# Attention maxima closed in bursts: the last reduction in one, the transpose between the matmuls of the next, with the maxima 45 steps ahead

## The chip, the cores and the metric

The kernel runs on one core of a Trainium2 chip. The metric is device time in microseconds (us) of one execution; where there are several runs, their median. Smaller is better.

## The reference

The input `x` is 2048 x 640 in float32. Three things are computed from it and mixed row by row:

```
qkv = x @ wqkv                      # 32 heads of 20
a   = softmax(q k^T / sqrt(20)) v   # per head, 2048 x 2048 scores
a   = a @ wo
b   = Re(DFT_seq(DFT_hidden(x)))    # = Cr @ (x Dr^T) - Ci @ (x Di^T)
g   = sigmoid(x . gate_w)
out = g * a + (1 - g) * b
```

## The kernel before, in words

**The work.** There are 16 pairs of heads and two halves of the queries, so 32 units (`NU`), each with two heads and 1024 queries. A unit takes 32 steps. The kernel computes the scores twice. In the maxima pass (`m`, `s_mm`, line 149) a step has two matmuls, one for each head (L159), whose 128 x 512 results VectorE reduces to their row maxima (L161). In the exponential pass (`e`, in `score`, line 664) a step has two matmuls of the transposed scores (L682), with the negated maxima as two extra rows of the query operand, and ScalarE takes their exponentials (L684). The unit's maxima must therefore be in the query operand before its first `e` step. A head uses 64 of the 128 partitions, so an `e` and an `m` matmul on different halves can run beside each other.

**Closing a unit's maxima.** After step 31 of a unit `s_end` (line 163) reduces the 64 partial maxima of a row block to 16 columns on VectorE (L167). At step 1 of the next unit it appends the unit to `chains`, and the next burst calls `max_chain` (line 187): TensorE transposes the 128 x 16 result (L190) into a PSUM bank, VectorE splits it into two parts (`split`, lines 102 and 103), and two steps later SyncE writes the parts to the extra rows of the query operand by four DMAs (lines 198 and 199).

**The prologue.** It projects q, k, v and the gate. 32 `qk_tile` calls (15 x 3 matmuls of 512 columns, L106 to L108, counted by `m`) are left when the maxima begin. Ahead of each third one, `segment` (line 313) computes one tile of the hidden transform (`hid_tile`, 15 pairs of half-height matmuls, L298) and four steps of the maxima pass beside it. `HEAD` is the number of these segments; `LEAD` the number of maxima steps done before the loop starts. The weights of a `qk_tile` are split by `fin()` at the second tile of each group of four.

**The loop.** It has 256 cycles; cycle `c` goes through `ORDER`: eight `e` and eight `m` matmuls, the filling `F`, and at the end the burst `B`. So the maxima pass runs `LEAD` steps ahead of the exponentials, and ends as many steps before the end of the loop. The filling is first the remaining `HID = 64 - HEAD` hidden tiles, one in a cycle, then three cycles with none, then the Fourier transform along the sequence: 56 units of 48 pairs of matmuls (L520), spread evenly over the cycles up to the last but one. The burst (line 688) runs due read-outs of the filling (`run_extras`), two steps of the product of exponentials and v (`av_step`, 8 matmuls each in the trace, L445), and then the chains that wait.

**Order.** Every engine does its instructions in the order in which this code issues them. `at_step(i, fn)` puts work at the begin of step `i` of the `e` pass. What matters here:

- `load_stack` (line 127) gives 12 DMAs for the k and q operands of the next pair of heads, four for k, four for each half of q. `begin` (line 628) puts them on GpSimd's queue (L632) at every second step from step 2 of a pair (64 steps) on. The first eight must have landed before the maxima pass reaches that pair.
- `unit_end` (line 450) copies the unit's output to `o` on ScalarE (L452), a single buffer, and places its normalising at later steps: 27 steps on, GpSimd multiplies (L477), 29 steps on, SyncE stores (L485). The next unit's copy waits for that store.
- `end` (line 644) issues `load_wb` for the weights of hidden tiles 32 to 47 and 48 to 63 when hidden tile 16 or 32 is due (`c + HEAD`), with GpSimd as the splitting engine; and the first loads of the Fourier stage by `HID`. The matrices `a` of that stage are loaded (`load_a`, six buffers `araw`) and split by GpSimd, two for each step from two steps after the last hidden tile on.
- PSUM banks for scores and transposes rotate over five (`bank`, line 112).

Of the kernel before, what the change touches and what calls it, by code (L numbers as in the profile page):

```python
# [10 lines left out]
F32 = mybir.dt.float32  # L11
R = mybir.dt.float32r
AF = mybir.ActivationFunctionType
ALU = mybir.AluOpType
AX = mybir.AxisListType
# [3 lines left out]
P = 128  # L19
# [5 lines left out]
NS = S // P  # L25
# [4 lines left out]
NU = 2 * NP  # L30
# [6 lines left out]
FIRST = {"e": (0, 0, 1, 1), "m": (1, 1, 1, 1)}  # L37


LEAD = 41  # L40
HEAD = 10

# [14 lines left out]
def f32(ap):  # L59
    return ap.bitcast(F32)  # L60
# [3 lines left out]
def mix_kernel(ctx: ExitStack, tc: tile.TileContext, xa, wqk, wb, cdft, wo, out):  # L64
    nc = tc.nc
    pe, act, dve, pool, sp = nc.tensor, nc.scalar, nc.vector, nc.gpsimd, nc.sync
    ctx.enter_context(tc.manual_schedule())

    def pools(**kw):
        return ctx.enter_context(tc.tile_pool(**kw))  # L70

    const = pools(name="const", bufs=1)
    small = pools(name="small", bufs=1)
# [24 lines left out]
    def split(dst1, dst2, src, e1, e2):  # L98
        if e1 is act:
            act.activation(dst1, src, AF.Copy)  # L100
        else:
            e1.tensor_copy(dst1, src)  # L102
        e2.tensor_tensor(dst2, src, f32(dst1), op=ALU.subtract)  # L103
# [8 lines left out]
    def bank():  # L112
        return ps_w.tile([P, 512], F32, name=f"ps{next(turn) % 5}")

    def pair_tile():
        return work.tile([P, 2, 512], F32, name="p", bufs=5)
# [10 lines left out]
    def load_stack(p):  # L127
        kt, qt = kst[p % 2], qst[p % 2]
        u = S // 2
        for t, o, two, one, cs in ((kt, D, 0, 2, slice(0, S)), (qt, 0, 1, 0, slice(0, u)), (qt, 0, 1, 0, slice(u, S))):  # L130
            for h in range(2):
                r = (2 * p + h) * DH
                b = 64 * h
                rows = slice(o + r, o + r + DH)
                yield f32(t[b + two * DH : b + (two + 2) * DH, cs]), qk_scr[:, rows, cs]
                yield f32(t[b + one * DH : b + (one + 1) * DH, cs]), qk_scr[0, rows, cs]

    def q_unit(n):
        u = n % 2 * (S // 2)
        return qst[n // 2 % 2][:, u : u + S // 2]  # L140

    mx, nms, chains = {}, {}, []
    now, later = [-1], {}

    def at_step(i, fn):
        later.setdefault(i, []).append(fn)
# [16 lines left out]
    def s_end(i):  # L163
        n, s = divmod(i, 32)
        if n < NU and s == 31:
            nms[n] = small.tile([P, 16], F32, name="nm", bufs=2)
            dve.tensor_reduce(nms[n], mx.pop(n).rearrange("p h q c -> p (h q) c"), axis=AX.X, op=ALU.max, negate=True)  # L167
        if s == 1 and 0 < n <= NU:
            if now[0] < 0:
                max_chain(n - 1)  # L170
            else:
                chains.append(n - 1)

    def s_step(i):
        for fn in [s_mm(i, h) for h in range(2)]:
# [11 lines left out]
    def max_chain(n):  # L187
        q = q_unit(n)
        pt = bank()[:16, :P]
        pe.transpose(pt, nms.pop(n), ident)  # L190
        m1 = small.tile([16, P], R, name="m1", bufs=2)
        m2 = small.tile([16, P], R, name="m2", bufs=2)
        split(m1, m2, pt, dve, dve)

        def rows():
            for h in range(2):
                b = 64 * h + KROWS
                sp.dma_start(f32(q[b : b + 1, :]), f32(m1[8 * h : 8 * h + 8, :]))
                sp.dma_start(f32(q[b + 1 : b + 2, :]), f32(m2[8 * h : 8 * h + 8, :]))

        if now[0] < 0:
            rows()
        else:
            at_step(now[0] + 2, rows)
# [16 lines left out]
    def load_wqk(c):  # L221
        raw = raw_tile()[:, : ND * P].rearrange("p (d c) -> p d c", d=ND)
        sp.dma_start(raw, wqk[c])

        def finish():
            w = part_tile().rearrange("p z c -> p (z c)")[:, : 2 * ND * P].rearrange("p (z d c) -> p z d c", z=2, d=ND)
            split(w[:, 0], w[:, 1], raw, act, dve)
            wt[c] = w

        return finish  # L230
# [19 lines left out]
    def flush(keep=0):  # L250
        while len(stores) > keep:
            sp.dma_start(*stores.pop(0))
# [60 lines left out]
    def segment(i, steps):  # L313
        def read_out(read, args):
            read()
            stores.append(args)

        tile_ = hid_tile(i, read_out)
        left = 3 * ND
        for k in range(steps):  # L320
            run_s(step + 1)
            for _ in range(left // (steps - k)):
                next(tile_)
                left -= 1
# [3 lines left out]
    def run_s(upto):  # L328
        nonlocal step
        while step < upto:  # L330
            s_step(step)
            step += 1
# [38 lines left out]
    for n, c in enumerate(order):  # L371
        for t in range(4):
            m = 4 * n + t
            if m % 3 == 0 and hid_done < HEAD:
                segment(hid_done, 4)
                hid_done += 1
            qk_tile(c, t)
            if t == 1:
                fin()
                if n + 2 < len(order):  # L380
                    fin = load_wqk(order[n + 2])
    run_s(LEAD)
    flush()
# [55 lines left out]
    def av_step(i, n, kt):  # L439
        v = vts[n // 2]  # L440
        pp = [pts.pop((n, kt, qc)) for qc in range(2)]
        for qc in range(2):
            for h in range(2):
                j = 2 * qc + h
                pe.matmul(av[32 * j : 32 * j + DH + 1, :], v[:, kt, h * (DH + 1) : (h + 1) * (DH + 1)],  # L445
                          pp[qc][:, h, :], start=kt == 0, stop=kt == NS - 1)
        if kt == NS - 1:
            unit_end(i, n)

    def unit_end(i, n):  # L450
        o = pa.tile([P, 512], F32, name="o")
        act.activation(o, av, AF.Copy)  # L452
        lc = pa.tile([P, 16], F32, name="lc")
        rb = pa.tile([P, 512], F32, name="rb")

        q = pool if n == NU - 1 else sp

        def store_l():
            for j in range(4):
                r = 32 * j + DH  # L460
                q.dma_start(l_scr[n, j : j + 1], o[r : r + 1, :])

        def load_l():
            q.dma_start(lc, l_scr[n].rearrange("j (a b) -> (j a) b", b=16))

        def recip():
            dve.reciprocal(lc, lc)

        def store_r():
            q.dma_start(r_scr[n].rearrange("j (a b) -> (j a) b", b=16), lc)  # L470

        def load_r():
            for j in range(4):
                q.dma_start(rb[32 * j : 32 * j + 32, :], r_scr[n, j : j + 1].to_broadcast([32, 512]))

        def norm():
            pool.tensor_tensor(o, o, rb, op=ALU.mult)  # L477

        def store_o():
            for qc in range(2):  # L480
                for h in range(2):
                    j = 2 * qc + h
                    t0 = (n % 2) * (S // 2) + qc * 512
                    r = (2 * (n // 2) + h) * DH
                    q.dma_start(o_scr[r : r + DH, t0 : t0 + 512], o[32 * j : 32 * j + DH, :])  # L485

        steps = (1, 5, 14, 16, 20, 27, 29) if n < NU - 2 else (1, 4, 10, 12, 15, 19, 21)
        for k, fn in zip(steps, (store_l, load_l, recip, store_r, load_r, norm, store_o)):
            if n == NU - 1:
                rest.append(fn)  # L490
            else:
                at_step(i + k, fn)
# [84 lines left out]
    def start_dft():  # L577
        flush()
        proj.release()
        apool.append(pools(name="apool", bufs=1))  # L580
# [19 lines left out]

    HID = 4 * NS - HEAD
    fills = itertools.chain(*(hid_tile(HEAD + g, read_later) for g in range(HID)), itertools.chain.from_iterable(dft_step(g) for g in range(NS * UNITS)))

# [24 lines left out]
    def begin(i):  # L628
        now[0] = i
        n, s = divmod(i, 32)  # L630
        for fn in later.pop(i, ()):
            fn()  # L632
        if s % 2 == 0:
            flush()
        if s == 0 and n % 2 == 0:
            p = n // 2
            if p + 1 < NP:
                at_step(i + 6, functools.partial(load_v, p + 1))
                for j, args in enumerate(load_stack(p + 1)):
                    at_step(i + 2 + 2 * j, functools.partial(pool.dma_start, *args))  # L640
        if i < total:
            pts[n, s // 2, s % 2] = pair_tile()

    def end(i):
# [3 lines left out]
        if i % 4 == 2:  # L648
            c = i // 4
            if c + HEAD in (NS, 2 * NS):  # L650
                load_wb(3 + (c + HEAD) // NS, pool, pool)()
            if c in (HID - 5, HID - 3):
# [8 lines left out]

    heads = {"e": 0, "m": 2 * LEAD}

    def score(kind):
        x = heads[kind]
        heads[kind] += 1
        i, z = divmod(x, 2)
        h = z ^ FIRST[kind][(i - (LEAD if kind == "m" else 0) - 1) % 4]
        if kind == "m":
# [17 lines left out]

    def burst(c):
        run_extras(max(done - HIDS, 0) // 3, 2)
        for kt in (2 * c, 2 * c + 1):  # L690
            av_step(now[0], kt // NS, kt % NS)
        while chains:
            max_chain(chains.pop(0))
        if c == HID - 1:
            start_dft()

# [89 lines left out]
```

## Time and profile before

| | |
|---|---|
| median of 3 runs | 1979.33 us (1977.02 to 1981.08) |
| the profiled execution | 1972.39 us |
| its span in the trace | 1970.6 us |
| TensorE (PE) busy | 1928.0 us, 98% |
| VectorE (DVE) busy | 1454.8 us, 74% |
| ScalarE (ACT) busy | 1212.2 us, 62% |
| GpSimd (POOL) busy | 1097.4 us, 56% |

A timeline row gives the start and the length in us, the engine, the line, the operation, `out<-in` with shapes, and the number of instructions merged. What stands in brackets is how long the engine was idle before it, and whose end ended that. A row of several instructions has the time from the first's start to the last's end. PE is matmuls, PEld their weight loads; SPq rows are DMA issues of SyncE. In the rows of groups the columns are busy us, mean ns, and the idle time before them.

### The profile page before, as it was taken

How to read it: one execution, taken by the hardware profiler on the slowest of the kernel's cores; microseconds unless marked ns; L12 is line 12 of the kernel's file. 1: busy time of each engine (PE TensorE's matmuls, PEld its weight loads, DVE VectorE, ACT ScalarE, POOL GpSimd, SP SyncE). 2: the span in 40 equal slices, each digit the busy share in tenths (PEclk: the TensorE clock that was granted, in tenths of full speed). 3: DMA queues.
4: the chain of work that ended last, by engine and by line, in shares of the span. 5: the costliest groups of instructions: out<-in, count | busy, mean ns of one | idle time of the engine just before them, and what ended most of it. 6: DMA issues, size and time to landing. Idle time of an engine off the chain costs nothing. (4 is left out here: it accounts for less than half of the span.)

```text
span 1970.6 us, 43800 instructions
## 1 busy us (share of the span) xinstructions
PE 1928.0 (98%) x17080; PEld 1384.3 (70%) x17080; DVE 1454.8 (74%) x2419; ACT 1212.2 (62%) x2337; POOL 1097.4 (56%) x1010
## 2 busy tenths in 40 slices
PE   8999999999999999999999999999999999999998
PEld 7987767767775666666676666666666666666678
DVE  4144569988887887888888878888888888888323
ACT  4221147767776666667776767677677666767741
POOL 1210001111004999756479987996686789787534
PEclk9999999999999999999999999999999999999999
DMA  7663321312114565436356646664555566553355
GB/s 222 172 170 132 131 91 46 84 51 72 51 51 133 181 195 161 121 111 159 101 152 191 194 151 186 195 191 125 153 175 137 172 182 184 147 169 128 102 158 177
DMA packets 196511, 281.02 MB, mean 143 GB/s; under 512 B 73373, under 2 KB 137917, under 8 KB 194385
## 3 DMA queue, kind: packets, MB, share of 16 engines
q1 hardware_dynamic: 158992, 246.20, 40.6%
q0 software_dynamic: 37312, 32.03, 6.5%
q8 instruction: 134, 2.20, 0.5%
q14 instruction: 73, 0.59, 0.1%
HBM read 213.81 MB, written 63.70 MB: 141 GB/s over the span
## 5 line engine op out<-in xcount | busy, mean ns | idle before, releaser
L161 DVE TENSOR_REDUCE mx<-ps 128x1 f32<-128x512 f32 x2048 | 1288.3, 684 | 210.4 <-PE ps L159 191.8
L684 ACT ACTIVATE p<-ps 128x512 f32<-128x512 f32 x2048 | 1081.0, 599 | 451.8 <-PE ps L159 244.4
L159 PE MATMUL ps<-kst,qst 60*128 60x512 f32 x2048 | 778.3, 428 | 19.6 <-ACT p L684 8.9
L682 PE MATMUL ps<-qst,kst 62*128 62x512 f32 x2048 | 705.2, 424 | 3.7 <-DMA qst<-m 2.2
L520 PE MATMUL yp<-a,part 64*128 64x320 f32 x5376 | 689.9, 310 | 0.1
L520 PEld LDWEIGHTS yp<-a,part 64*128 64x128 f32 x5376 | 595.2, 187 | 15.5 <-DVE m L540 0.3
L445 PE MATMUL av<-p,v 128*21 128x512 f32 x4096 | 493.3, 597 | 0.1
L682 PEld LDWEIGHTS ps<-qst,kst 62*128 62x128 f32 x2048 | 339.1, 185 | 212.6 <-DVE mx L161 179.3
L159 PEld LDWEIGHTS ps<-kst,qst 60*128 60x128 f32 x2048 | 366.0, 185 | 51.2 <-ACT p L684 12.3
L103 POOL TENSOR_TENSOR part<-raw,part 128x1024 fp32r<-128x1024 f32 x112 | 267.3, 2387 | 9.0
L445 PEld LDWEIGHTS av<-p,v 128*21 128x21 f32 x4096 | 98.2, 100 | 226.3 <-issue 222.7
L298 PE MATMUL yp<-wb,xs 64*128 64x320 f32 x1920 | 239.8, 312 | 2.1 <-ACT raw L306 1.9
L298 PEld LDWEIGHTS yp<-wb,xs 64*128 64x128 f32 x1920 | 208.9, 189 | 7.1 <-ACT raw L306 2.5
L416 POOL TENSOR_TENSOR raw<-raw,raw 128x1024 f32<-128x1024 f32 x78 | 187.8, 2408 | 9.4 <-DMA raw<-in_cdft 9.1
L551 POOL TENSOR_TENSOR yt<-yt,m 128x320 f32<-128x320 f32 x64 | 56.2, 879 | 146.9 <-DVE m L540 146.6
L102 POOL CAST wb<-raw 128x966 fp32r<-128x966 f32 (+1 forms) x4 | 3.4, 856 | 228.6 <-DMA raw<-in_wb 196.7
L102 POOL CAST part<-raw 128x1024 fp32r<-128x1024 f32 x112 | 116.3, 1039 | 18.3 <-PE yp L520 12.5
L477 POOL TENSOR_TENSOR o<-o,rb 128x512 f32<-128x512 f32 x32 | 41.5, 1296 | 133.7 <-DMA rb<-r_scr 131.5
L103 POOL TENSOR_TENSOR a<-araw,a 128x320 fp32r<-128x320 f32 x112 | 97.7, 872 | 9.0
L103 DVE TENSOR_TENSOR p<-ps,p 128x512 fp32r<-128x512 f32 x40 | 27.5, 691 | 94.9 <-ACT p L100 92.1
L106 PE MATMUL ps<-xs,part 128*128 128x512 f32 x200 | 80.3, 402 | 7.5 <-ACT xs L100 6.2
L100 ACT ACTIVATE p<-ps 128x512 fp32r<-128x512 f32 x40 | 23.8, 597 | 102.5 <-PE ps L108 102.4
(68 smaller groups left out, 1389.0 us busy)
## 6 DMA issues: line engine op xcount, KB each, us to landing
raw<-in_cdft SPq DMA_DIRECT2D x192, 512.0 KB
araw<-a_scr SPq DMA_DIRECT2D x192, 160.0 KB
qk_scr<-p SPq DMA_DIRECT2D x40, 512.0 KB
y_scr<-yt SPq DMA_DIRECT2D x96, 160.0 KB
kst<-qk_scr POOLq DMA_DIRECT2D x32, 320.0 KB, 14.1
qst<-qk_scr POOLq DMA_DIRECT2D x64, 160.0 KB, 8.7
a_scr<-raw SPq DMA_DIRECT2D x64, 160.0 KB
yt<-y_scr SPq DMA_DIRECT2D x64, 160.0 KB
```

Source lines behind the costliest of these rows:

```text
L102: e1.tensor_copy(dst1, src)
L103: e2.tensor_tensor(dst2, src, f32(dst1), op=ALU.subtract)
L106: pe.matmul(ps, st1, mv1, start=first, stop=False)
L159: pe.matmul(ps, q[b : b + KROWS, qt * P : (qt + 1) * P], k[b : b + KROWS, kc * 512 : (kc + 1) * 512], start=True, stop=True)
L161: return lambda: dve.tensor_reduce(mx[n][:, h, qt, kc : kc + 1], ps, axis=AX.X, op=ALU.max)
L298: pe.matmul(yp[h][:, :HE], xs[r, xz, d, cs], w[r, wz, d, :HE], start=d == 0 and z == 0, stop=d == ND - 1 and z == 2)
L416: pool.tensor_tensor(raws[0], raws[0], raws[1], op=ALU.add if PRODUCTS[n][0][1][0] > 0 else ALU.subtract)
L445: pe.matmul(av[32 * j : 32 * j + DH + 1, :], v[:, kt, h * (DH + 1) : (h + 1) * (DH + 1)], pp[qc][:, h, :], start=kt == 0, stop=kt == NS - 1)
L520: pe.matmul(yp[h][:, :HE], c[r, cz, cs], a[r, az], start=s == 0 and z == 0, stop=s == NS - 1 and z == 2)
L551: pool.tensor_tensor(y, y, m, op=ALU.add if sg > 0 else ALU.subtract)
L682: pe.matmul(pt, k[b : b + KROWS + 2, kt * P : (kt + 1) * P], q[b : b + KROWS + 2, qc * 512 : (qc + 1) * 512], start=True, stop=True)
L684: act.activation(pts[n, kt, qc][:, h], pt, AF.Exp, scale=float(DH) ** -0.5)
```

## The change

`LEAD` goes from 41 to 45 and `HEAD` from 10 to 11, so one more segment stands in the prologue, and one hidden tile fewer in the loop. The closing reduction becomes a function of its own, `max_nm`; in the loop `s_end` only notes that the unit is due (`ends`). The next burst calls `max_nm` ahead of its matmuls and, one step later, moves the unit to `chains`, so that the burst after it calls `max_chain`, now between its two `av_step`s instead of after them. With the pass 45 steps ahead, the unit's last maxima come one cycle earlier than before, and the transpose falls into the same burst (after step 24 of the unit in the `e` pass) as before. The 12 loads of `load_stack` are placed 1.5 steps apart, from step 2 to step 18 instead of 24.

```
-LEAD = 41
-HEAD = 10
+LEAD = 45
+HEAD = 11
...
     def s_end(i):
         n, s = divmod(i, 32)
         if n < NU and s == 31:
-            nms[n] = small.tile([P, 16], F32, name="nm", bufs=2)
-            dve.tensor_reduce(nms[n], mx.pop(n).rearrange("p h q c -> p (h q) c"), axis=AX.X, op=ALU.max, negate=True)
-        if s == 1 and 0 < n <= NU:
             if now[0] < 0:
-                max_chain(n - 1)
+                max_nm(n)
             else:
-                chains.append(n - 1)
+                ends.append(n)
+        if s == 1 and 0 < n <= NU and now[0] < 0:
+            max_chain(n - 1)
+
+    def max_nm(n):
+        nms[n] = small.tile([P, 16], F32, name="nm", bufs=2)
+        dve.tensor_reduce(nms[n], mx.pop(n).rearrange("p h q c -> p (h q) c"), axis=AX.X, op=ALU.max, negate=True)
...
-                    at_step(i + 2 + 2 * j, functools.partial(pool.dma_start, *args))
+                    at_step(i + 2 + 3 * j // 2, functools.partial(pool.dma_start, *args))
...
     def burst(c):
         run_extras(max(done - HIDS, 0) // 3, 2)
-        for kt in (2 * c, 2 * c + 1):
-            av_step(now[0], kt // NS, kt % NS)
+        while ends:
+            max_nm(ends[0])
+            at_step(now[0] + 1, functools.partial(chains.append, ends.pop(0)))
+        av_step(now[0], 2 * c // NS, 2 * c % NS)
         while chains:
             max_chain(chains.pop(0))
+        av_step(now[0], (2 * c + 1) // NS, (2 * c + 1) % NS)
```

2 lines of the change are left out of this document (1 added, 1 removed).

## Prediction

> **What bounds the kernel now.** I read the page first, for the busy shares.
>
> ```profile
> span 1970.6 us, 43800 instructions
> PE 1928.0 (98%) x17080; PEld 1384.3 (70%) x17080; DVE 1454.8 (74%) x2419; ACT 1212.2 (62%) x2337; POOL 1097.4 (56%) x1010
> L161 DVE TENSOR_REDUCE mx<-ps 128x1 f32<-128x512 f32 x2048 | 1288.3, 684 | 210.4 <-PE ps L159 191.8
> ```
>
> TensorE is never seen idle for long, yet its matmuls overlap, so 98% does not say that it sets the pace. The timeline does. The loop has 256 cycles; each ends in a burst of 16 L445 matmuls, so the distance between two L445 rows is the length of a cycle. In the Fourier stage, where a cycle is filled with 12 or 16 pairs of L520 matmuls, I took one stretch of each kind:
>
> ```profile
> 1384.49 1.92 PE L445 MATMUL av<-p,v 128*21 128x512 f32 x16
> 1390.73 1.91 PE L445 MATMUL av<-p,v 128*21 128x512 f32 x16
> ...
> 1397.04 1.91 PE L445 MATMUL av<-p,v 128*21 128x512 f32 x16
> 1403.11 1.47 PE L445 MATMUL av<-p,v 128*21 128x512 f32 x10
> ```
>
> ```profile
> 1026.96 1.92 PE L445 MATMUL av<-p,v 128*21 128x512 f32 x16
> 1033.33 1.91 PE L445 MATMUL av<-p,v 128*21 128x512 f32 x16
> ...
> 1039.84 1.91 PE L445 MATMUL av<-p,v 128*21 128x512 f32 x16
> 1046.12 1.47 PE L445 MATMUL av<-p,v 128*21 128x512 f32 x9
> ```
>
> The first stretch has 12 pairs a cycle, the second 16. The plain cycles (the last of each) take 6.07 and 6.28 us: four more pairs cost only 0.21 us. Something else than TensorE's work limits the 12-pair cycle. VectorE's timeline shows what:
>
> ```profile
> 1389.44 0.22 DVE L167 TENSOR_REDUCE nm<-mx 128x16 f32<-128x64 f32 x1
> ...
> 1399.45 4.98 DVE L161 TENSOR_REDUCE mx<-ps 128x1 f32<-128x512 f32 x8 [1.10 <-PE ps L682]
> ```
>
> The eight maxima of a cycle run end to end for 4.98 us, then VectorE rests 1.10 us, while TensorE is in its burst and makes no scores. So a cycle is a chain: maxima back to back, then the burst. **Whatever VectorE does between two maxima is paid; what it does during the burst, up to that rest, is not; and whatever lengthens the burst is paid.** Where no maxima are left, at the end of the loop, a 12-pair cycle takes 4.74 us:
>
> ```profile
> 1846.86 1.92 PE L445 MATMUL av<-p,v 128*21 128x512 f32 x16
> 1851.60 1.91 PE L445 MATMUL av<-p,v 128*21 128x512 f32 x16
> ```
>
> **The change, part by part.** Times are against the profiled execution, 1972.39 us (span 1970.6), which is 6.94 us under the median of the three runs, 1979.33. I work out a difference and add it to the median.
>
> *The closing reduction (L167) moves into a burst.* The row 1389.44 lies inside the cycle 1384.49 to 1390.73, which is 6.24 long against 6.07 plain: 0.17. With 16 pairs: 1026.96 to 1033.33 is 6.37 against 6.28: 0.09. With a hidden-transform tile (15 L298 pairs) as filling:
>
> ```profile
> 299.06 1.92 PE L445 MATMUL av<-p,v 128*21 128x512 f32 x16
> 305.31 1.91 PE L445 MATMUL av<-p,v 128*21 128x512 f32 x16
> 311.67 1.91 PE L445 MATMUL av<-p,v 128*21 128x512 f32 x16
> ```
>
> 6.36 against 6.25: 0.11. In the burst it stands behind the last maxima, and even where the read-out of a tile shares that rest, 0.42 us of it is left:
>
> ```profile
> 307.72 2.61 DVE L161 TENSOR_REDUCE mx<-ps 128x1 f32<-128x512 f32 x4 [0.42 <-PE ps L159]
> ```
>
> So its 0.22 is covered; without that cover it would cost what it costs now. How often it runs:
>
> ```profile
> L167 DVE TENSOR_REDUCE nm<-mx x32: 220/220/221, 222.3 to 1840.5; 128x16 f32<-128x64 f32 x32
> ```
>
> Of the 32, the first stands in the prologue, and the last ones touch the end of the maxima or one of the disturbed cycles below; I count 29, by the filling of their cycles: 14 x 0.17 + 8 x 0.09 + 7 x 0.11 = **-3.9 us**.
>
> *The transpose (L190) goes between the two steps of the burst.* Today its cycle, 1390.73 to 1397.04, takes 6.31 against 6.07, with 16 pairs 6.51 against 6.28. In the new place its wait for the reduction is gone, but that wait was not what ended last. TensorE's weight loads around one transpose:
>
> ```profile
> 834.48 0.12 PEld L445 LDWEIGHTS av<-p,v 128*21 128x21 f32 x4 [0.31 <-issue]
> 834.90 0.12 PEld L445 LDWEIGHTS av<-p,v 128*21 128x21 f32 x4 [0.31 <-issue]
> 835.87 0.09 PEld L190 LDWEIGHTS ps<-ident,nm 128*16 128x16 f32 x1 [0.85 <-DVE mx L161]
> 836.08 0.18 PEld L682 LDWEIGHTS ps<-qst,kst 62*128 62x128 f32 x1
> ```
>
> Inside the burst the loads come every 0.42 us, one group of four ahead, so the last group starts at about 835.33. The transpose's load is not drawn ahead: it comes 0.54 after that, 0.12 later than a next group would. It holds TensorE for 0.21. (The maximum named as releaser was long done; the load stands behind the burst.) Between the two steps there are two such ends of a group train instead of one, so I add 0.11 to the 0.21: burst 0.43 + 0.54 + 0.21 + 0.43 + 0.54 = 2.15 against 2.04. VectorE's two copies of the transpose then fall into its rest, but today's 6.31 is 0.24 over plain, of which TensorE's 0.21 is nearly all, so little is gained. 31 transposes x 0.11 = **+3.4 us**. The bounds: -0.9 (31 x the 0.03 of the copies, if the place itself were free) and +6.5 (the whole 0.21 once more).
>
> The Trainium skill ("TensorEngine Tiling (Array Packing)", Key Properties) says that a change of tiling mode drains the engine; by it the edit adds one drain per unit, and the 0.12 above agrees with that.
>
> *The eleventh segment.* A hidden-transform tile and four steps of maxima move from the loop into the prologue. What a segment costs there, and what stands at the place where the new one goes (ahead of tile 30 of 32):
>
> ```profile
> 215.70 0.40 PE L108 MATMUL ps<-xs,part 128*128 128x512 f32 x1
> ...
> 220.31 0.50 PE L106 MATMUL ps<-xs,part 128*128 128x512 f32 x1
> ...
> 220.89 0.39 PE L108 MATMUL ps<-xs,part 128*128 128x512 f32 x1
> ```
>
> ```profile
> 260.74 0.40 PE L108 MATMUL ps<-xs,part 128*128 128x512 f32 x1
> 262.45 0.50 PE L106 MATMUL ps<-xs,part 128*128 128x512 f32 x1 [1.31 <-ACT part L100]
> ...
> 263.31 0.51 PE L108 MATMUL ps<-xs,part 128*128 128x512 f32 x1
> ```
>
> These matmuls follow each other at 0.23, so a segment adds 220.31 - 215.70 - 0.23 = 4.38. At the new place TensorE already waits for weights that ScalarE and VectorE are still splitting: 262.45 - 260.74 - 0.23 = 1.48, and 0.28 more at 263.31 (0.86 from the restart against 0.58 at 220.31). The segment covers that: 4.38 - 1.76 = **+2.6**.
>
> In the loop one hidden cycle (6.25) becomes a Fourier cycle. 199 of them instead of 198 share the same 56 units of 48 pairs; units take 3 cycles of 16 or 4 of 12, so 78 sixteen-pair cycles become 75: 6.07 - 3 x 0.21 - 6.25 = **-0.8**. The maxima end a cycle earlier, so one more cycle runs without them: 4.74 - 6.07 = **-1.3**.
>
> *The filling moved a cycle earlier against the units.* The longest cycle of the hidden stage:
>
> ```profile
> 417.57 0.91 SPq L237 DMA_DIRECT2D raw<-in_wb  x2
> ...
> 427.87 1.42 SPq L485 DMA_DIRECT2D o_scr<-o  x4
> ```
>
> ```profile
> 421.17 0.99 POOL L102 CAST wb<-raw 128x966 fp32r<-128x966 f32 x1 [31.91 <-PE ps L159]
> ...
> 426.55 1.29 POOL L477 TENSOR_TENSOR o<-o,rb 128x512 f32<-128x512 f32 x1
> ```
>
> ```profile
> 425.02 1.92 PE L445 MATMUL av<-p,v 128*21 128x512 f32 x16
> ...
> 430.64 0.60 ACT L452 ACTIVATE o<-av 128x512 f32<-128x512 f32 x1 [4.17 <-DMA o_scr<-o]
> ...
> 431.78 0.49 PE L159 MATMUL ps<-kst,qst 60*128 60x512 f32 x1 [3.21 <-ACT p L684]
> ...
> 436.39 1.06 PE L445 MATMUL av<-p,v 128*21 128x512 f32 x8
> ```
>
> Read backwards: TensorE waits for an exponential, ScalarE for the store of the unit's output `o`, the store for GpSimd's normalising (L477), and that stood behind GpSimd's split of weights, whose load went out at 417.57. The cycle takes 11.37, 5.1 over 6.25. With one tile fewer in the loop, `load_wb` comes four steps (6.2 us) earlier, the normalising stays at its step, and GpSimd's 5.4 us of splitting end before it. **-5.1 us**; between -5.1 and 0.
>
> *The stack loads (L632) at 1.5 steps instead of 2.* The eighth, the last that the next pair's first maximum needs, goes from step 16 to 12, and that maximum from 23 to 19: seven steps both times. I cost it at zero, but GpSimd must reach the place four steps sooner; the last rival prices that.
>
> Sum: -3.9 + 3.4 + 2.6 - 0.8 - 1.3 - 5.1 = **-5.1 us**: 1974.2 on the median, 1967.3 for an execution like the profiled one.
>
> **Rivals.**
>
> *The transpose is free between the steps* (chance 0.12). Its load could be drawn under the first step and the second step's under the transpose. Against it: neither its load nor the scores' load behind it is drawn ahead in the rows above. Then the 3.4 goes, and with the hidden copies 0.9 more: 1969.9. The Trainium skill ("TensorE: Matmul & The Clock Gate", Part 2) says that loads into the background weight buffer are pulled ahead of running matmuls; that would give this case.
>
> *The long wait only moves* (0.16). At the start of the Fourier stage, also a cycle earlier, a unit's output store comes in SyncE's queue behind 14 loads of `araw` instead of six, and these wait for GpSimd to free six buffers. If that delays ScalarE there as the weights did, 5 us come back: 1979.3, no change.
>
> *Slower: GpSimd reaches the stack loads too late* (0.22). Today this already happens:
>
> ```profile
> 620.65 2.78 POOL L632 DMA_DIRECT2D qst<-qk_scr  x5
> ...
> 623.14 0.54 PE L159 MATMUL ps<-kst,qst 60*128 60x512 f32 x1 [2.28 <-DMA qst<-qk_scr]
> ```
>
> GpSimd takes its instructions in order and each load costs it 0.56; eight in 10 steps instead of 14, among its splits. The load landed 2.5 us after its issue; from there every us of lateness is a us of TensorE. If GpSimd is busy without a rest, moving a load past four steps of its work brings it forward by less than 6.2 us. A shortfall of 1 us in each of the 12 pairs of the Fourier stage gives +12: 1986. It decides when the eighth load is issued under 2.5 us ahead of the pair's first maximum.
>
> **How the numbers follow.** The forecast has 0.50, the rivals 0.12, 0.16 and 0.22. A measurement here tells about 0.2% (4 us) from no change. The forecast lies just beyond it; its own range is 1968 to 1980 (the transpose at its bounds, the weights' stall between gone and half left), so of its 0.50 I give 0.32 to faster, 0.16 to same, 0.02 to slower. The free transpose is faster, the moved wait 0.11 same and 0.05 slower, the late loads slower save 0.01. Together: faster 0.44, same 0.28, slower 0.28. The range from 1965 to 1988 reaches from the free transpose, a little further, to the late loads.
>
> **What would show it.** Right: L167 inside the burst and its cycle at plain length; a burst with the transpose about 2.15 us up to the next score's load; no wait of TensorE near 262; the split of `wb` over before L477, and no 11-us cycle there. Wrong: second-step L445 loads ahead of the transpose's end; an 11-us cycle a few cycles into the Fourier stage; waits on `qst<-qk_scr` longer and in more pairs than now.

## The result: about 17 us slower, and the profile after

The changed kernel takes 1994.95 us (median of 6 runs, 1992.62 to 1999.29) against 1977.74 us for the kernel before, run beside it (6 runs, 1971.16 to 1981.08). The ratio is 1.0098 (95% interval 1.0076 to 1.0120). The profiled execution took 1993.63 us, 21.2 more than the one shown of before. In the code after, lines up to 165 keep their numbers and those quoted from later on move by 3, apart from the closing reduction: `av` is L448, the exponentials L687, the stack loads L635, the transpose L193; the closing reduction is L175.

From the page of the changed kernel (busy time and share by engine; two groups, whose columns are busy us, mean ns, idle time before them and what ended most of it):

```profile
PE 1939.0 (97%) x17080; PEld 1380.6 (69%) x17080; DVE 1457.1 (73%) x2419; ACT 1211.4 (61%) x2337; POOL 1097.1 (55%) x1010
L161 DVE TENSOR_REDUCE mx<-ps 128x1 f32<-128x512 f32 x2048 | 1289.7, 685 | 240.0 <-PE ps L159 221.5
L159 PE MATMUL ps<-kst,qst 60*128 60x512 f32 x2048 | 780.3, 430 | 34.7 <-DMA qst<-qk_scr 18.6
```

The work is the same: VectorE's maxima take 1289.7 us as they took 1288.3. What grew is the idle time before them, from 210.4 to 240.0, and the last row names a cause at the end of the chain: L159 itself, the matmuls of the maxima pass, waited for a DMA of the stacks.

The timeline says where in the span the time was lost. The loop's first burst starts at 282.24 us after and at 280.35 before, so in these two executions 1.9 us are lost ahead of the loop. From the first burst to the last the loop takes 1628.70 us against 1608.56, 20.1 more; after it the kernel gains 0.9. To split the loop I took the length of each of its 256 cycles, the median of each kind (filling, with or without the reduction or the transpose), and what single cycles lie over the median of their kind. That excess is 49.1 us after and 29.6 before. **So 19.5 of the loop's 20.1 us are in some 16 disturbed cycles, and the other 240 are as long as before within a few us in all.**

Of the waits of TensorE (total us, times, longest), these name them. After, then before:

```profile
PE ps L159 <- DMA qst<-qk_scr: 18.6, 4, 6.9
PE ps L159 <- DVE mx L161: 10.1, 7, 3.2
```

```profile
PE ps L159 <- DMA qst<-qk_scr: 4.6, 3, 2.3
```

Four long waits for `qst`, the query half of a pair's stack, stand at the first maximum of pairs 4, 9, 11 and 14 (counted from 0):

```profile
617.11 0.76 PE L159 MATMUL ps<-kst,qst 60*128 60x512 f32 x1 [6.91 <-DMA qst<-qk_scr]
...
1132.53 0.76 PE L159 MATMUL ps<-kst,qst 60*128 60x512 f32 x1 [4.35 <-DMA qst<-qk_scr]
...
1347.82 0.76 PE L159 MATMUL ps<-kst,qst 60*128 60x512 f32 x1 [3.66 <-DMA qst<-qk_scr]
...
1653.88 0.76 PE L159 MATMUL ps<-kst,qst 60*128 60x512 f32 x1 [3.65 <-DMA qst<-qk_scr]
```

At the first maximum of a pair TensorE waits 18.9 us in all, against 7.0 before: +11.9. The cycles there and the ones behind them lie 32.1 us over their medians, against 10.3: +21.8. All other disturbed cycles together: 17.0 after, 19.3 before. Of the 21.8, some 20 are the stack loads': the four waits above and the cycles behind them cost 27.8, the three waits for `qst` in the kernel before 7.6. Of the other cycles there, after the change 4.2 us (pairs 5, 8 and 10) come behind a wait of VectorE's for the sums of the softmax. This is the loss, and the rest of the document is about two questions: why the loads come late, and why 11.9 us of waiting cost 21.8.

**One pair, read closely.** GpSimd's issues of the stack loads of pair 9, after and before. The eight that the first maximum needs are the four of `kst` and the first four of `qst`:

```profile
1106.72 1.25 POOL L635 DMA_DIRECT2D kst<-qk_scr  x2
1110.30 0.66 POOL L635 DMA_DIRECT2D kst<-qk_scr  x1
...
1116.88 0.53 POOL L635 DMA_DIRECT2D kst<-qk_scr  x1
1117.40 0.64 POOL L635 DMA_DIRECT2D qst<-qk_scr  x1
1121.18 1.69 POOL L635 DMA_DIRECT2D qst<-qk_scr  x3
```

```profile
1107.47 1.25 POOL L632 DMA_DIRECT2D kst<-qk_scr  x2
1111.01 1.18 POOL L632 DMA_DIRECT2D kst<-qk_scr  x2
1120.44 1.17 POOL L632 DMA_DIRECT2D qst<-qk_scr  x2
1124.76 0.65 POOL L632 DMA_DIRECT2D qst<-qk_scr  x1
1131.35 0.53 POOL L632 DMA_DIRECT2D qst<-qk_scr  x1
```

The issue of the eighth ends 9.0 us earlier after the change (1122.87 against 1131.35 plus 0.53), as intended. It lands at 1132.53, when TensorE's wait ends: only 1.4 us before the 1133.90 at which the first maximum ran before. From the first issue to the eighth landing it takes 25.8 us. The place of the first load is step 2 both times, and the first maximum stands at step 64 - LEAD: 21 steps behind the first load with LEAD 41, 17 with 45. A step is a quarter of a cycle, 1.56 us: **32.8 us of room before, 26.5 after, of which GpSimd's lateness takes 5** (step 2 of the pair began at 1101.77).

The same sum holds for the other pairs of the Fourier stage. In pairs 9, 11 and 14 GpSimd issues the first load 5.0, 4.8 and 3.9 us behind the begin of step 2, so that 21.5, 21.7 and 22.6 us are left, and the eight need 25.6, 25.1 and 26.0 until they have landed: these three wait. In pair 5 GpSimd is as late (5.1), but there the cycle before had already lost 3.2 us, and only 0.3 of waiting are left. In the other pairs from 6 on it is at most 2.2 us late, the eight take 20.6 to 26.8 us, and TensorE does not wait.

**Pair 4, with the longest wait, is another case.** It lies where the Fourier matrices begin. GpSimd issued its first load at 577.07, and then stood before the sum of two such matrices (L419), which waited for its data:

```profile
577.07 0.67 POOL L635 DMA_DIRECT2D kst<-qk_scr  x1 [16.87 <-PE ps L159]
590.35 2.40 POOL L419 TENSOR_TENSOR raw<-raw 128x1024 f32<-128x1024 f32 x1 [12.61 <-DVE mx L161]
...
596.25 1.67 POOL L635 DMA_DIRECT2D kst<-qk_scr  x3
...
609.86 3.38 POOL L635 DMA_DIRECT2D qst<-qk_scr  x6
```

The eighth is the second of the last row, issued at 610.50, when TensorE was ready for the first maximum since 610.20 (617.11 - 6.91). Here the place of the first load says little; GpSimd came too late to the others. In the kernel before the same stand cost 2.28 us of waiting (623.14, a row of the prediction). So 4.6 of the 11.9 us are pair 4's.

**What a long gap costs beyond itself.** By windows of the changed kernel around the same wait (stretch; its length and the busy us of PE, PEld, DVE, ACT and POOL; then the granted clock, the DMA engines' busy share, GB/s):

```profile
1120.00:1128.00 8.00, 8.00 (x78) 5.88 (x74) 6.90 (x13) 6.01 (x13) 7.77 (x10) 1.00 0.81 220
1132.50:1134.50 2.00, 1.97 (x12) 2.00 (x14) 1.17 (x2) 0.00 (x0) 1.94 (x4) 0.50 0.49 103
...
1140.00:1148.00 8.00, 8.00 (x81) 5.70 (x79) 7.47 (x15) 5.97 (x13) 7.86 (x6) 1.00 0.27 88
```

```profile
1123.54 1.92 PE L448 MATMUL av<-p,v 128*21 128x512 f32 x16
1135.17 3.16 PE L448 MATMUL av<-p,v 128*21 128x512 f32 x16
1142.50 1.06 PE L448 MATMUL av<-p,v 128*21 128x512 f32 x8
```

After the gap TensorE runs on half the clock: the burst takes 3.16 us where it took 1.92. The cycle with the wait takes 11.63, 5.55 over the 6.08 of its kind, and the next one 7.33, 1.22 over: 6.8 us for a gap of 4.35. The first row shows something else: while the eight loads were under way, the DMA engines were busy for 81% and moved 220 GB/s. The Trainium skill ("TensorE: Matmul & The Clock Gate", Part 1) says that the clock falls to half after an idle window of about 3.4 us and rises again after as long a busy one; the 0.50 after gaps of 3.65 to 6.91 us and the 1.00 from 1140 on agree. But 3.4 us is no threshold here: shorter gaps were followed by half the clock too, the one of 2.42 us before 717.24 by 0.50 from 717.9 to 721.3, and in the kernel before that of 2.28 us before 623.14 by 0.50 from 623.4 to 626.8. Over the four pairs the cycles lost 27.8 us (8.4, 6.8, 5.9 and 6.7) for 18.6 us of gaps.

### The profile page after: what moved, and what is told of

Read it like the earlier page. It is cut to its first block, busy times and chain, and to the rows that moved or that the text cites. A ratio compares the mean times of both kernels' runs of the same rounds, so it can differ in the third digit from the quotient of the medians.

```text
span 1991.7 us, 43795 instructions
## 1 busy us (share of the span) xinstructions
PE 1939.0 (97%) x17080; PEld 1380.6 (69%) x17080; DVE 1457.1 (73%) x2419; ACT 1211.4 (61%) x2337; POOL 1097.1 (55%) x1010
## 5 line engine op out<-in xcount | busy, mean ns | idle before, releaser
L161 DVE TENSOR_REDUCE mx<-ps 128x1 f32<-128x512 f32 x2048 | 1289.7, 685 | 240.0 <-PE ps L159 221.5
L687 ACT ACTIVATE p<-ps 128x512 f32<-128x512 f32 x2048 | 1080.4, 599 | 479.8 <-PE ps L159 251.2
L159 PE MATMUL ps<-kst,qst 60*128 60x512 f32 x2048 | 780.3, 430 | 34.7 <-DMA qst<-qk_scr 18.6
L448 PE MATMUL av<-p,v 128*21 128x512 f32 x4096 | 508.0, 607 | 0.1
L159 PEld LDWEIGHTS ps<-kst,qst 60*128 60x128 f32 x2048 | 366.5, 186 | 67.5 <-issue 23.7
L448 PEld LDWEIGHTS av<-p,v 128*21 128x21 f32 x4096 | 95.9, 101 | 216.6 <-issue 209.0
L419 POOL TENSOR_TENSOR raw<-raw,raw 128x1024 f32<-128x1024 f32 x78 | 187.8, 2408 | 13.6 <-DMA raw<-in_cdft 9.7
L102 POOL CAST part<-raw 128x1024 fp32r<-128x1024 f32 x112 | 116.4, 1039 | 23.4 <-PE yp L523 18.0
L103 DVE TENSOR_TENSOR p<-ps,p 128x512 fp32r<-128x512 f32 x40 | 27.5, 691 | 92.2 <-ACT p L100 89.5
L635 POOL DMA_DIRECT2D qst<-qk_scr x120 | 69.4, 591 | 28.8 <-DMA kst<-qk_scr 27.5
## 6 DMA issues: line engine op xcount, KB each, us to landing
kst<-qk_scr POOLq DMA_DIRECT2D x32, 320.0 KB, 15.7
```

What stands on the lines that cost most here:

```text
L159: pe.matmul(ps, q[b : b + KROWS, qt * P : (qt + 1) * P], k[b : b + KROWS, kc * 512 : (kc + 1) * 512], start=True, stop=True)
L161: return lambda: dve.tensor_reduce(mx[n][:, h, qt, kc : kc + 1], ps, axis=AX.X, op=ALU.max)
L419: pool.tensor_tensor(raws[0], raws[0], raws[1], op=ALU.add if PRODUCTS[n][0][1][0] > 0 else ALU.subtract)
L687: act.activation(pts[n, kt, qc][:, h], pt, AF.Exp, scale=float(DH) ** -0.5)
```

## The experiments

**My theory**, once the traces lay side by side: the lead (45) takes four steps from the time between the first stack load and the first maximum, and the 25 us that eight loads need no longer fit. Its rival: the new spacing of the loads is the culprit, since it crowds GpSimd's queue. Others: the transpose in the burst costs more than the rows of before showed; the reduction in the burst delays the transpose. Times are medians, each against runs of the kernel before on the same chip, whose median was 1973.9 to 1974.8 in these sessions.

**1. The lead alone** (kernel before):

```
-LEAD = 41
-HEAD = 10
+LEAD = 45
+HEAD = 11
```

> The kernel before with the maxima 45 steps ahead and eleven segments, and nothing else: closing and transpose as before, loads of the next pair of heads every second step. Theory A (headroom): the eight loads that a pair's first maximum needs take some 25 us from the first issue at step 2; with 19 steps instead of 23 until they are needed, TensorE waits. Here the eighth is placed at step 16, only three steps before, so the waits on these loads are at least those of the change (excess of disturbed cycles 49 us there, 30 before), and the kernel is 15 to 40 us slower than before. Theory B (density): the loads 1.5 steps apart are what delays; then this kernel has no more waits on them than before and lies within 5 us of it, on the fast side by the 5 us of the weights' stall. Theory C (the filling moved by a cycle): the waits lie elsewhere than at a pair's first maximum.

Measured: 2051.55 us, ratio 1.0385 [1.0363, 1.0407]: 77 us slower.

```profile
PE ps L159 <- DMA qst<-qk_scr: 64.8, 10, 11.8
```

The lead, with the eleventh segment that goes with it here, is the culprit, and far beyond what I expected of it (15 to 40 us); experiments 9 and 10 take the two apart. TensorE waits 68.6 us at the pairs' first maxima, and the excess of disturbed cycles is 104.1 us.

**2. The change with the old spacing of the loads:**

```
-                    at_step(i + 2 + 3 * j // 2, functools.partial(pool.dma_start, *args))
+                    at_step(i + 2 + 2 * j, functools.partial(pool.dma_start, *args))
```

> The changed kernel with the loads of the next pair at every second step again, all else changed. Theory A: worse than the change by 5 to 30 us, since the eighth load comes at step 16 for a first maximum at step 19. Theory B: back to the kernel before or below it (0 to -5 us).

Measured: 2059.32, ratio 1.0426 [1.0404, 1.0449]. The denser spacing is no cause of the loss: it takes 64 us of it back.

**3. The new spacing alone** (the kernel before with `3 * j // 2`).

> The kernel before with the loads 1.5 steps apart and nothing else: maxima still 41 steps ahead, first needed at step 23. Theory A: the loads have seven steps more than in the change after the last of the eight; no wait on them longer than before, some shorter: 0 to -10 us. Theory B: 10 to 20 us slower, as the change.

Measured: 1968.16, ratio 0.9969 [0.9954, 0.9983]. At the old lead the denser loads are a gain of some 6 us; TensorE's waits at the pairs' first maxima fall from 7.0 us to 0.4. The rival is out.

**4. The transpose between the `av` steps, alone:**

```
-        for kt in (2 * c, 2 * c + 1):
-            av_step(now[0], kt // NS, kt % NS)
+        av_step(now[0], 2 * c // NS, 2 * c % NS)
         while chains:
             max_chain(chains.pop(0))
+        av_step(now[0], (2 * c + 1) // NS, (2 * c + 1) % NS)
```

> The kernel before with the transpose between the two steps of the burst instead of after them; the closing reduction stays where it was. If the second end of a group train costs 0.13 us for each of 31 transposes, as the changed trace suggests: +4 us (3 to 5), the transpose's cycle 0.12 to 0.13 longer than in the kernel before. If the longer transpose cycle of the change has another cause (the reduction's new place), 0 to 1 us.

Measured: 1978.42, ratio 1.0018 [1.0005, 1.0031]: 3.6 us slower. Its cycles with a transpose take 6.57, 6.43 and 6.64 us (hidden tile, 12 pairs, 16 pairs) where the kernel before takes 6.45, 6.31 and 6.52: 0.12 each, 31 times 3.7.

**5. The reduction in a burst, alone** (the transpose stays behind the burst):

```
     def burst(c):
+        while ends:
+            max_nm(ends.pop(0))
         run_extras(max(done - HIDS, 0) // 3, 2)
```

> The kernel before with the closing reduction at the head of the burst in whose cycle the unit ends, and the transpose after the two steps of that same burst as before; maxima 41 steps ahead, loads as before. If the reduction is covered by VectorE's rest in the burst: its cycles at plain length (6.10 instead of 6.25 with 12 pairs, 6.25 instead of 6.37 in the hidden stage), -4 us (-3 to -5) by the undisturbed cycles. Rival: the transpose in the same burst now waits for the reduction, which stands behind the last maxima; then its cycle grows by 0.3 us or more and the sum is +5 us or more.

Measured: 1971.32, ratio 0.9985 [0.9964, 1.0006], some 3 us faster, though the interval touches no change. What it says for sure is in the cycles: those with the reduction take 6.24, 6.09 and 6.31, which is the plain length; those with the transpose are unchanged.

**6. The changed kernel with the loads still denser** (`i + 1 + j`: one in each step, from step 1 on).

> The changed kernel with the 12 loads at every step from step 1 on (eighth at step 8 instead of 12). If the wait is set by when the eighth load is issued (lateness of GpSimd): the waits at a pair's first maximum go, excess of disturbed cycles from 49 to some 25 us, -20 us against the change, at or under the kernel before. If it is set by a fixed time of some 25 us from the first issue to the eighth landing: only the one step by which the first comes earlier is gained, 1.6 us a pair where it waits, -5 to -12 us against the change, still above the kernel before.

Measured: 1998.86, ratio 1.0118 [1.0084, 1.0151]: no gain, where both branches of the expectation had one. Pair 9 again, GpSimd's issues and the first maximum, and then GpSimd's and TensorE's waits:

```profile
1109.14 2.39 POOL L635 DMA_DIRECT2D kst<-qk_scr  x4
...
1120.44 1.69 POOL L635 DMA_DIRECT2D qst<-qk_scr  x3
```

```profile
1134.58 0.76 PE L159 MATMUL ps<-kst,qst 60*128 60x512 f32 x1 [3.98 <-DMA qst<-qk_scr]
```

```profile
POOL qst L635 <- DMA kst<-qk_scr: 86.2, 39, 7.9
```

```profile
PE ps L159 <- DVE mx L161: 19.7, 8, 6.7
PE ps L159 <- DMA qst<-qk_scr: 9.8, 3, 4.1
```

The four of `kst` go out without a pause, and the eighth lands 25.4 us after the first issue, against 25.8 with the wider spacing. **In the Fourier stage some 25 us is what the eight loads need, and no spacing of mine made it shorter** (medians over pairs 5 to 15: 25.4 in the changed kernel, 25.7 here, 30.8 with two steps' spacing in experiment 1). Nor does the first load go out earlier for its earlier place: in pair 9 it is again 5.0 us behind the begin of step 2. What the dense spacing does instead is to hold GpSimd: a load waits for an earlier one to land, 86.2 us in all against 27.5 in the changed kernel, and the splits and read-outs behind it come late. The waits at the pairs' first maxima fall to 9.8, and others rise as much.

**7. The loads on SyncE's queue** (`sp.dma_start` in place of `pool.dma_start`, in the changed kernel).

> The changed kernel with the 12 loads on SyncE's queue instead of GpSimd's, at the same steps. If the time to land comes of GpSimd's own queue and of its lateness: the eighth lands under 6 us after its issue, no waits at a pair's first maximum, excess from 49 to 25 us or less. If the transfers themselves are what takes 10 us (the DMA engines are shared): same landing times, same waits. If SyncE comes too late to them because it stands behind stores that wait: the waits move to other places or grow.

Measured: 2094.64, ratio 1.0596 [1.0555, 1.0636], the slowest of all.

```profile
PE ps L159 <- DMA qst<-qk_scr: 48.3, 13, 5.3
PE ps L159 <- DVE mx L161: 47.8, 14, 6.3
```

The time is no answer: as I read it, what a stack load waits for on SyncE the matrix stream and the stores behind it wait for too, and the second row shows waits that are not for the stacks at all. SyncE also takes 20 to 30 us to issue the eight, where GpSimd takes 13 (median). But from the eighth's issue to the first maximum, at which TensorE waits in every pair from 5 to 15, it is 10.5 us (median; 7.7 to 12.2), and in the changed kernel the eighth lands 10.6 us after its issue (median; 9.1 to 14.8). So the landing is as slow on this queue, which speaks against GpSimd's queue as the cause. It is not a clean test, since the matrix stream is in SyncE's queue as well.

**8. The kernel before with the two parts that gain**: loads at 1.5 steps, reduction in the burst; lead 41, ten segments, transpose behind the burst (the edits of 3 and 5).

> The kernel before with two parts of the change that cost nothing there: loads 1.5 steps apart (measured alone: ratio 0.997) and the reduction in the burst, transpose after both steps, maxima 41 steps ahead, ten segments. If the two add up: -6 -4 = -10 us against the kernel before, ratio 0.995, about 1964.

Measured: 1965.93, ratio 0.9949 [0.9931, 0.9966]. Faster than both kernels.

**9. The same with eleven segments**, the last with one step of maxima in place of four, so that the lead stays 41.

> The kernel before with three parts of the change: loads 1.5 steps apart, the reduction in the burst, and an eleventh segment that takes a hidden tile out of the loop but only one step of maxima with it, so that the maxima stay 41 steps ahead; transpose after both steps. Against the kernel with the first two (ratio 0.995 to before): the cycle in which GpSimd's split of weights held up the normalising (5 us over) should be plain, the segment costs about 2 in the prologue and gives back 0.8 in the loop: -3 to -5 us more, about 1962, ratio 0.993. Rival: the filling a cycle earlier brings other waits of the Fourier stage and nothing is left: ratio 0.995 or above.

Measured: 1971.39, ratio 0.9982 [0.9970, 0.9994], so the eleventh segment loses 5 us here. The weights' cycle of 11.4 us is gone, as intended: the bursts there start at 416.49, 422.75 and 429.06. But waits come up elsewhere. One kind comes with the eleventh segment: VectorE waits in the loop for the sums of the softmax (`lc<-l_scr`) here, in experiment 10 and in the changed kernel (7.6 us in three places there), and in none of the kernels with ten segments. The first two rows of TensorE's waits, where experiment 8 has 6.3 us for exponentials and 1.7 for maxima:

```profile
PE ps L159 <- ACT p L690: 14.1, 6, 4.8
PE ps L159 <- DVE mx L161: 9.6, 6, 3.2
```

The excess of disturbed cycles is 33.9 us against 23.4. So moving the filling by one cycle against the units removes one meeting of GpSimd, a store and ScalarE, and others come up; which stream makes each of them I did not test.

**10. The changed kernel with a lead of 43**; the eleventh segment has three steps of maxima, the others four:

```
-LEAD = 45
+LEAD = 43
...
-                segment(hid_done, 4)
+                segment(hid_done, 4 if hid_done < 10 else 3)
```

> The changed kernel with the maxima 43 steps ahead instead of 45, all else changed; the last segment has three steps. The first maximum of a pair then comes at step 21, 19 steps (29.7 us) after the loads' place. If some 25 us of transfers and up to 5 us of GpSimd's lateness are what has to fit: the waits nearly go, excess of disturbed cycles from 49 to 30 or less, -15 to -22 us against the change, near the kernel before. If the waits come with the eleventh segment or the new place of closing: no change against the changed kernel.

Measured: 1975.57, ratio 1.0004 [0.9990, 1.0017], 19 us back.

```profile
PE ps L159 <- DMA qst<-qk_scr: 3.8, 3, 2.9
```

The eight loads take 25.2 us as before. Two steps, 3.1 us more of room, and the waits at the pairs' first maxima fall from 18.9 to 4.0, of which 2.95 are pair 4's. This is the sharpest test of the theory. Between the two profiled executions 17.3 us of the gain lie in the loop and 2.9 ahead of it. From experiment 9 (lead 41, 0.9982) to here the transposes add their 3.6 us (experiment 4, 0.0018), and within the intervals that is all the difference: from 41 to 43 the lead costs nothing that I can see, and from 43 to 45 some 19 us.

**11. Less traffic beside the loads**: the changed kernel with the second matrix of the two-term products not loaded.

> The changed kernel, which leaves out the second load of a Fourier matrix where a product has two terms (the first is added to itself, so the output is another): 112 loads of the matrix instead of 192, same work on every engine. If the eight loads take 25 us because they share the DMA engines with that stream (in the hidden stage, with little of it, they take 15 to 17): the time from first issue to the eighth landing falls to 20 us or less in those products and the waits at a pair's first maximum go or halve, -8 to -20 us against the change. If it is GpSimd's queue alone: same 25 us, same waits, 0 to -3 us.

Measured: 1963.12, ratio 0.9934 [0.9910, 0.9959]. Two rows of its DMA view, with the packets, MB and share of the queue that carries the matrices and the median from issue to landing, and the same two of the changed kernel:

```profile
q1 hardware_dynamic: 147472, 204.25, 34.8%
...
kst<-qk_scr POOLq DMA_DIRECT2D x32, 320.0 KB, 13.7
```

```profile
q1 hardware_dynamic: 158992, 246.20, 40.5%
...
kst<-qk_scr POOLq DMA_DIRECT2D x32, 320.0 KB, 15.7
```

With 42 MB less to carry, the eight loads land 22.5 us after the first issue in place of 25.4, the waits at the first maxima fall from 18.9 to 6.7 (4.75 of them in pair 4), and the excess from 49.1 to 18.7, at a lead of 45. The time to land fell less than the expectation said (20 or less). So a part of the 25 us is shared DMA time. Other transfers get faster as well, so the gain in time need not be all the stack loads'.

**12. Experiment 8 with the normalising and the store one step earlier** (steps 26 and 28 in place of 27 and 29), so that GpSimd comes to it before the weights.

> The kernel before with loads 1.5 steps apart, the reduction in the burst, maxima 41 steps ahead and ten segments (ratio 0.995), and the normalising and the store of a unit's output one step earlier, 26 and 28 instead of 27 and 29. In GpSimd's order the normalising then stands ahead of the split of the second hidden weights instead of behind it. If that order alone made the 11.4 us cycle of the hidden stage, its 5 us go without moving the filling; the later waits of ScalarE for the same store shrink by up to a step each: -5 to -8 us more, ratio 0.991 to 0.993, about 1960. If the store itself is late for another reason: the 11.4 us cycle stays and the ratio is 0.995.

Measured: 1963.78, ratio 0.9942 [0.9925, 0.9959]. The order is turned round: GpSimd normalises at 406.28 and begins the split of the weights at 421.84. The 11.4 us cycle is gone, and the kernel is no faster than experiment 8 within the intervals: other cycles lie higher (5.7 at one, 4.3 at another). It is the fastest complete version that I have, with experiment 8 beside it.

## Why the prediction was wrong, by its own steps

**The step that failed is "I cost it at zero"**: the stack loads, "seven steps both times". The prediction measured from the eighth load's place to the first maximum, and took the landing from one row of before: issued at 620.65, landed at 623.14. Seven steps are 10.9 us, and that leaves 8.4 to spare. But that load was alone: in that pair its seven forerunners had landed by 617.5. In pairs 7, 9 and 11 of before the eighth went out 4 us or more behind the seventh and landed as fast (2.35 to 2.53 us); in the other pairs from 5 on, where it followed within 0.8 us, it took 6.1 to 11.2. After the change, where it goes out among its neighbours, it takes 10.6 us (median of pairs 5 to 15), and nothing is left to spare. The quantity that counts is then the time from the *first* issue, 25.4 us (median of the same pairs). Before the change it hardly showed, since the issues themselves, two steps apart and late, were spread over as long: 30.5 us from the first issue to the eighth landing, in a room of 32.8. The right sum would have set 25 us and 5 of lateness against 26.5. The trace of before had the numbers: its DMA view gives a median of 14.1 us from issue to landing for the 320 KB loads of `kst`, and I took 2.5. The Trainium skill ("DMA: Bandwidth & Descriptors", Anatomy of one DMA) puts a load on this queue at 2.0 us plus its bytes at 436 GB/s. By it I estimate 2.75 us for the 320 KB loads and 2.2 for one of 80 KB, as the eighth is; medians of 14.1 and 15.7 for the first do not agree, and only the lone eighth, with 2.4, comes near.

The other steps:

- **The reduction, -3.9.** Right. It runs behind the last maxima of the cycle (878.07, below), and its cycle, 876.84 to 882.94, has the plain 6.10. Over the kinds (hidden tile, 12 pairs, 16 pairs) its cycles lost 0.13, 0.15 and 0.06, which makes -3.5 over the 29.

```profile
876.84 1.91 PE L448 MATMUL av<-p,v 128*21 128x512 f32 x16
...
882.94 1.06 PE L448 MATMUL av<-p,v 128*21 128x512 f32 x8
883.93 0.28 PE L193 MATMUL ps<-ident,nm 128*16 128x128 f32 x1
884.13 1.05 PE L448 MATMUL av<-p,v 128*21 128x512 f32 x8
885.12 0.49 PE L685 MATMUL ps<-qst,kst 62*128 62x512 f32 x1
...
889.37 1.92 PE L448 MATMUL av<-p,v 128*21 128x512 f32 x16
```

```profile
875.67 2.48 DVE L161 TENSOR_REDUCE mx<-ps 128x1 f32<-128x512 f32 x4
878.07 0.21 DVE L175 TENSOR_REDUCE nm<-mx 128x16 f32<-128x64 f32 x1
879.26 4.99 DVE L161 TENSOR_REDUCE mx<-ps 128x1 f32<-128x512 f32 x8 [0.98 <-PE ps L159]
```

- **The transpose, +3.4.** Right. From the burst's begin to the next score it takes 2.18 us (882.94 to 885.12; forecast 2.15), and its cycles grew by 0.12 to 0.13, which makes 3.9 over 31; alone, in experiment 4, 3.6 us. The rival that has it free is out: the second step's first row, at 884.13, stands behind the transpose.
- **The eleventh segment, +2.6.** Too small. The first burst comes only 1.9 later, but the stretch ahead of the first segment, which the change leaves alone, happened to be 2.0 shorter in this execution (the first hidden tile starts at 109.93 against 111.89). From there to the first burst it is 172.3 us against 168.5, 3.8 more. That stretch is 168.4 to 168.5 in the six kernels with ten segments and a lead of 41, and 171.6 to 172.3 in the six with eleven and 45, so 3.1 to 3.9. The wait near 262 that the segment was to cover is gone, as forecast.
- **The hidden cycle, -0.8, and the cycle without maxima, -1.3.** Too small to be told apart: the undisturbed cycles sum to 0.6 more than before, where the reduction and the transpose alone would nearly cancel, and the stretch after the loop is 0.9 shorter.
- **The weights' stall, -5.1.** The mechanism is right: GpSimd ends its splits before it comes to the normalising, and the cycles there take 6.25 (bursts at 401.70, 407.95 and 414.20).

```profile
418.31 1.34 POOL L103 TENSOR_TENSOR wb<-raw,wb 128x644 fp32r<-128x644 f32 x1
419.61 1.30 POOL L480 TENSOR_TENSOR o<-o,rb 128x512 f32<-128x512 f32 x1
```

But the gain did not stay. Away from the pairs' first maxima the disturbed cycles sum to 17.0 us against 19.3, so of 5.1 some 2.3 are left. The rival "the long wait only moves" was right in this, though not by the place that it named: the waits are spread over the Fourier stage. The longest in the changed kernel are VectorE's, for the sums of the softmax, and ScalarE's, for the store of `o`:

```profile
1230.85 0.25 DVE L470 RECIPROCAL lc<-lc 128x16 f32<-128x16 f32 x1 [3.27 <-DMA lc<-l_scr]
```

```profile
1265.88 0.60 ACT L455 ACTIVATE o<-av 128x512 f32<-128x512 f32 x1 [4.36 <-DMA o_scr<-o]
```

- **The rival "GpSimd reaches the stack loads too late"** is what happened at the place it named, but by its condition in pair 4 alone, where the eighth issue comes 0.3 us behind TensorE. In the others its condition did not hold. It set the eighth issue 2.5 us ahead of the maximum as the point that decides; in pair 9 TensorE was ready at 1128.18 (1132.53 - 4.35), 5.3 us after the eighth issue, and the load was late all the same. That its price of 12 us is near the 11.9 of added waiting is luck: it stood for 1 us in each of 12 pairs, and there are four waits of 3.65 to 6.91. What it left out is what follows a long gap, the half clock above all, and with that the cost at the first maxima is 21.8.

Against the 1967.3 us that the prediction gave for an execution like the profiled one, 1993.63 is 26.3 more. Of these, 21.8 stand at the pairs' first maxima, some 20 of them the stack loads', and 2.8 are the stall's return (5.1 forecast, 2.3 left); the segment was 1.2 too little and the transpose 0.5, and the shorter start gives back 2.0. Some 2 us I can't place: a hundredth in the median of 240 cycles would do it.

What stays open: how much of the 25 us is the loads' own and how much is sharing. Experiment 11 shows that sharing is a part (2.9 us for 42 MB). In pairs 2 and 3, in the hidden stage, the eight take 15 to 17 us even though they go out within 4 us, and there the DMA engines are less busy (58% from 375 to 392, where pair 2's are under way, against 90% from 1106.7 to 1132.3 in pair 9). So most of the time is there without the Fourier stage's matrices. Experiment 7 speaks against GpSimd's queue; what else makes it I don't know.

## What to carry to other kernels

Where a consumer needs a group of transfers, measure from the first issue to the last landing of the group, in the stage where it will run, and set that against the time between the first issue and the consumer; the place of the last issue alone says little, and one that landed alone says nothing of the others. When a pass is made to run further ahead, its loads' *first* place must move ahead as well, or the lead is paid for by the loads (this follows from the sum of room and landing; no run here moved the first place by more than a step). Look also at what stands ahead of the loads in the issuing engine's order, since in pair 4 that made the longest wait. Count a long gap of TensorE at half as much again (27.8 us for 18.6 here), since the clock falls behind it, and expect an edit that shifts one stream against another to trade the waits it can see for waits that it can't.

## What the runs showed of the hardware that I had not expected

- Eight loads on GpSimd's queue, 80 to 320 KB each, take 15 to 17 us from first issue to last landing in the hidden stage and 25 in the Fourier stage (median), at a spacing of 1.5 steps and of one; with two steps it is 30.8. A lone eighth takes 2.35 to 2.53.
- After gaps of 3.65 us and more, and also after two of 2.28 and 2.42, the granted clock was 0.50; a burst of 1.92 us then took 3.16. Four gaps of 18.6 us in all cost 27.8.
- A transpose between two groups of `av` matmuls costs 0.12 us more than behind both, in every kind of cycle.
